# Fewer and larger transfers on the SP queue of an attention-then-mixture kernel, and V's transposed copy loaded one pair sooner

## The chip, the cores and the metric

One core of one Trainium2 chip runs the whole kernel as one program. The metric is the device time of one execution in microseconds (us), measured without the profiler, as the median of several runs. One further execution was profiled; all rows below come from it.

## The reference

Causal attention over 8 batches of 12 heads, 448 positions, head size 64; its rows (3584 tokens of 768 numbers) go through a mixture of 8 experts. Each token goes to the expert with its largest gate logit, each expert keeps its 80 tokens of highest gate weight, and all other rows of the output are zero.

```python
scores = q @ k.T / 8                      # (8, 12, 448, 448), causal mask
attn = exp(scores - max) / (sum + 1e-9)
x = (attn @ v) as rows of (8*448, 12*64)
logits = x @ w_gate                        # 8 experts
e = argmax(logits); g = softmax(logits)[e]
for each expert: its at most 80 tokens of largest g:
    out[token] = g * (relu(x[token] @ w1[e]) @ w2[e])     # 768 -> 1024 -> 768
```

## The kernel before

**Attention** runs over 48 pairs of heads (8 batches of 6 pairs; the two heads of a pair lie on partitions 0 to 63 and 64 to 127). The loop over pairs `i` has 8 slots `k`, and `CYCLE` writes down what each slot issues: the scores of pair `i` (`sp`, TensorE), their masking and minimum (`ns`, `nb`, VectorE), the exponentials (`prob`, ScalarE), the transposes of pair `i-1` (`tp`, copied to `PT`), the product with the values of pair `i-2` (`xo`, scaled to `xr` by VectorE in slot 5), and the store of pair `i-3` (`st`, slot 0) into the scratch tensor `xs`. Everything runs in the order in which it is written (`manual_schedule`), on each engine by itself. A group of three pairs is a half batch (`PH` = 3).

**Loads.** `load_pair` brings q and k of pair `i+4` in slot 0, each as its own transfer, into the raw tile `qk` (three pairs in rotation, `RING`); `split_pair` on GpSimd (POOL) makes two 16-bit parts of pair `i+3` in slot 6 (L344 a cast, L346 two subtractions). `load_values` brings the values `vt` of the next half batch. `load_turned` brings V a second time, with positions along the free dimension (`vT`): 672 KB in each of the pairs `p` = 4 and 5 of a batch, for the batch after the next.

**What vT is for.** The gate's logits come out of the attention product itself: V times the gate weights (`gp`, L377, TensorE) is put beside V. For a batch from the third on, this product is planned in the batch before it, with `gp0` in pair 1, slot 4 and `gp1` in pair 2, slot 4 (`FOLD`: 12 and 20 slots). There is one `vT` tile, so its next load waits for `gp1`. For the second batch, `FOLD_SECOND` plans `gp1` in pair 4, slot 4 of the first (36 slots).

**The turn of a batch.** Choosing the experts and ranking the tokens of batch `b` is spread over the two batches behind it (`STEPS`, in slots after the batch's end). At 55 comes `rank` (POOL), at 59 `rr` (VectorE, reads `rank`), at 60 `tn` (TensorE, reads `rr`) and then `tab` (VectorE, reads `tn`). Slot 60 is pair 1, slot 4 as well, so on TensorE `gp0` stands right ahead of `tn`, and `tn` right ahead of the scores of the next pair. This text calls that place the turn.

**Fill.** From pair 5 on, slots 1, 4 and 7 each issue one more transfer: a part of a piece of the expert weights (`piece_parts`, 192 or 256 KB, tile `wraw`) or, when no piece is due (`LOADS`), 64 zero rows of the output (`zero_rows`, 192 KB, out of the zero columns of `mask`).

**The queue.** Nearly all transfers are issued by SP in one program order, 414 of them. They take eight completion semaphores in turn (DMAHW0 to DMAHW7), so each issue first waits until the transfer eight before it has landed.

**The end.** `TAIL` orders the last values, gate and ranking steps; `close` clears the three tiles `xg0` to `xg2`, which take the gathered rows. Then the experts run, with weights in 1.5 MB transfers, and each expert's rows are scattered into the output.

Of the kernel before, what the change touches and what calls it, by code (L numbers as in the profile page):

```python
# [7 lines left out]
F32 = mybir.dt.float32  # L8
# [9 lines left out]
P = 128  # L18
DH = 64
# [3 lines left out]
TILES = 7  # L23
# [18 lines left out]

TAIL = """
st v0 ta tb rest2 ya yb sums0 lgp0 rows0 st0 rest6 v1 turned close rest4 sums1 lgp1 piece logit shifted raised *2 chosen rows1
st1 sums one_hot wsum one_zero wmore columns r0t r0c *3 weight weighted parts hold rl r1t r1c *1 lt cp ro
c3w c3l c2w c2l c1w gt3 *2 c0w c1l gt2 *1 c0l *1 gt1 places *1 earlier gt0 places_more own *5 rank rr tn tab *28
"""

# [2 lines left out]
def attention_then_moe(  # L51
    ctx: ExitStack,
    tc: tile.TileContext,
    qT: bass.AP,
    kT: bass.AP,
    v: bass.AP,
    vT: bass.AP,
    wg: bass.AP,
# [4 lines left out]
    capacity: int,  # L63
):
    nc = tc.nc
    B, _, NP, S = qT.shape
    N, D = out.shape
    E = wg.shape[2]
    F = w1.shape[3]
# [18 lines left out]
    spool = sel_stack.enter_context(tc.tile_pool(name="sel", bufs=2, side="right"))  # L88
# [38 lines left out]
    for r in range(2):  # L127
        x = akeep.tile([P, P * sum(CHUNKS)], F32, name=f"prob{r}")
# [7 lines left out]
    PH = NP // HB  # L136
    v_bufs = []
    for r in range(2):
        t = akeep.tile([P, NT, 2 * PH * VW], F32, name=f"vt{r}")
# [11 lines left out]
    PW = 3072  # L151
# [23 lines left out]
    wmore = [wearly]  # L175
# [21 lines left out]
    def piece_parts():  # L197

        got = []
        k = PIECES[len(wload)][3]  # L200
        got.append(piece())
        half = PW // k // 2

        def part(j, x):
            t, src = got[0]
            nc.sync.dma_start(t[:, j, x * half:(x + 1) * half], src[:, j, x * half:(x + 1) * half])
        return [lambda j=j, x=x: part(j, x) for j in range(k) for x in range(2)]


    presplits = [], [], []  # L210
# [25 lines left out]
    for r in range(2):  # L236
        t = akeep.tile([P, NT, H, E + 1], F32, name=f"fold{r}")
# [4 lines left out]
    zero = mask[:, 0:D // 2]  # L242
    zdone = [0]
    xg_bufs = []
# [68 lines left out]
    def zero_rows():  # L313

        r0 = zdone[0]
        n = min(P // 2, N - r0)
        nc.sync.dma_start(out[r0:r0 + n, :].rearrange("r (h c) -> (r h) c", h=2), zero[0:2 * n, :])
        zdone[0] += n


# [1 line left out]
    lo, hi = slice(0, DH), slice(DH, P)  # L322

    def raw_of(i):

        x = qk_raw[:, i % RING * 2 * S:(i % RING + 1) * 2 * S]
        return x, x[:, 0:S], x[:, S:2 * S]
# [5 lines left out]

    def load_pair(i):
        b, p = divmod(i, NP)
        _, q, k = raw_of(i)
        nc.sync.dma_start(q, qT[b, :, p, :])
        (nc.sync if i else nc.scalar).dma_start(k, kT[b, :, p, :])

    def split_pair(i):  # L340

# [16 lines left out]
    def load_turned(b, p0, p1):  # L358

        if b not in turned_values:  # L360
            turned_values[b] = akeep.tile([P, NP, S], F32, name="vT")
        nc.sync.dma_start(turned_values[b][:, p0:p1, :], vT[b, :, p0:p1, :])
# [111 lines left out]
    def values_group(pr):  # L474
        st = state[pr.b * HB + pr.p // PH]
        p = pr.p % PH

        def work():
            xo = pr.xo = ps_u.tile([P, 2, 512], F32, name="xo", tag="u")[:, 0, 0:TILES * VW].rearrange("k (t w) -> k t w", w=VW)
# [26 lines left out]
                                    in1=pr.r.unsqueeze(2).to_broadcast([P, TILES, E]), op=ALU.mult)  # L506

        def rows():
            xr = pr.xr = spool.tile([P, TILES, DH], F32, name="xr", tag="xr", bufs=4)
            nc.vector.tensor_tensor(out=xr, in0=pr.xo[:, :, 0:DH], in1=pr.r.unsqueeze(2).to_broadcast([P, TILES, DH]),  # L510
                                    op=ALU.mult)

        def store():
            xr = pr.xr
            r0, c0 = pr.b * S, pr.p * P
            nc.sync.dma_start(xs[r0:r0 + NO * P, c0:c0 + P].rearrange("(t k) d -> k t d", k=P),
                              xr[:, 0:2 * NO, :].rearrange("k (t j) d -> k t (j d)", j=2))
            for j, of in enumerate((lo, hi)):
                nc.sync.dma_start(xs[r0 + NO * P:r0 + S, c0 + j * DH:c0 + (j + 1) * DH], xr[of, TILES - 1, :])
        return work, sums, logits, rows, store  # L520

    NO = NT - 1
# [378 lines left out]
    with tc.manual_schedule():  # L901
# [25 lines left out]
        for i, pr in enumerate(pairs):  # L927
# [17 lines left out]
            for k in range(SLOTS):  # L945
# [15 lines left out]
                    load_values((i + 1) // PH)  # L961
                if i == 2 and k in (2, 5):
                    load_turned(1, k - 2, k + 1)
                if bt.b < B - 2 and k == 6 and pr.p >= NP - 2:
                    load_turned(bt.b + 2, 3 * (pr.p - NP + 2), 3 * (pr.p - NP + 3))

                if i == n - 2 and k == 0 and len(wload) >= WBUF and not parts:
                    load_piece()
# [3 lines left out]
                        f()  # L972
                        todo.remove(f)

                if i > 4 and k in (1, 4, 7):
                    if not parts and len(wload) < WBUF and (not PRE or i >= LOADS[len(wload)]):
                        parts = piece_parts()
                        if len(wload) <= PRE:
                            presplit(len(wload) - 1)
                    if parts:  # L980
                        parts.pop(0)()
                    elif zdone[0] < N:
                        zero_rows()
# [31 lines left out]
        def close():  # L1015
            att.close()
            wmore.append(ctx.enter_context(tc.tile_pool(name="wmore1", bufs=1, reuse_waits="tile")))
            xg_pool = ctx.enter_context(tc.tile_pool(name="xg", bufs=1, reuse_waits="tile"))
            for i in range(3):
                t = xg_pool.tile([SL, D], F32, name=f"xg{i}")  # L1020
                (nc.gpsimd if i else nc.vector).memset(t, 0.0)
                xg_bufs.append(t)
        steps["close"] = close

        def keep_warm(times):
# [342 lines left out]
```

## Time and profile before

| | |
|---|---|
| median of 3 runs | 456.21 us (454.61 to 457.66) |
| profiled execution | 456.73 us, span of its records 455.0 us |
| attention, about | 0 to 320 us |
| last ranking and first gather, about | 320 to 346 us |
| experts, about | 346 to 455 us |
| TensorE, VectorE, ScalarE, GpSimd busy | 398.4, 354.3, 341.0, 223.6 us |

Times in rows are us from the start of the span. A stretch's DMA share is the mean busy share of the core's 16 DMA engines. In a timeline, the bracket behind a row is the time that the engine sat idle ahead of it and what ended it.

### The profile page before, as it was taken

The page shows a single profiled execution, that of the slowest core. Times are in us where ns is not written, and L with a number is a line of the kernel's source. Part 1 is how long each engine was busy: PE and PEld are TensorE (multiplying, and loading weights), DVE is VectorE, ACT ScalarE, POOL GpSimd, SP SyncE. Part 2 cuts the span into 40 slices and gives each one's busy share as a digit, 9 for nine tenths or more (in the row PEclk, how much of TensorE's full clock was granted, in tenths as well). Part 3 has the DMA queues.
Part 4 walks back from the last instruction along what each step waited for, and adds up shares of the span by engine and source line. Part 5 has one row for each costly group of instructions (what it writes and reads, how often), then busy time and mean ns, then how long its engine had stood idle before and what let it go on. Part 6 is the DMA issues. An engine that isn't in the chain of part 4 may idle for free.

```text
span 455.0 us, 21917 instructions
## 1 busy us (share of the span) xinstructions
PE 398.4 (88%) x9186; PEld 350.8 (77%) x9187; DVE 354.3 (78%) x1321; ACT 341.0 (75%) x622; POOL 223.6 (49%) x362
## 2 busy tenths in 40 slices
PE   5699889798969989995997998898697889999994
PEld 3488778687848868883887787788367889999993
DVE  5366789687947879883698679988776999999792
ACT  5589779778848887982797688885744599897791
POOL 5665567477757857675675565631160241200002
PEclk9999999999979999996899899999699999999998
DMA  8948988979988798998889796456539999999911
GB/s 290 363 139 265 284 249 264 321 224 287 282 287 269 229 325 248 295 264 279 283 265 296 253 292 192 136 167 210 169 100 351 409 396 395 388 414 426 408 46 43
DMA packets 66034, 122.89 MB, mean 270 GB/s; under 512 B 13282, under 2 KB 54242, under 8 KB 62608
## 3 DMA queue, kind: packets, MB, share of 16 engines
q1 hardware_dynamic: 64736, 117.76, 76.1%
q0 software_dynamic: 1056, 3.51, 2.5%
q8 instruction: 72, 1.18, 1.1%
q14 instruction: 26, 0.21, 0.1%
q10 hardware_dynamic: 144, 0.23, 0.1%
HBM read 97.91 MB, written 23.99 MB: 268 GB/s over the span
## 4 chain that ended last, share of the span: by engine, by line
PE 53%; DMA 19%; DVE 13%; issue 6%; POOL 4%; SPq 3%; ACT 0%; POOLq 0%; DVEq 0%
PE xo L485 11%; PE sp L431 9%; DMA vT<-v_d 8%; PE tp L463 6%; DMA xs<-xr 5%; DVE ns L441 5%; PE op L1167 3%; PE op L1159 3%; PE hp L1173 3%; PE hp L1174 3%; PE hp L1171 3%; DMA xg<-xs,idx 3%; PE gp L377 2%; DMA qk<-k_t 2%; POOL qk L346 2%
## 5 line engine op out<-in xcount | busy, mean ns | idle before, releaser
L448 ACT ACTIVATE prob<-ns,nb 128x448 f32<-128x448 f32 (+6 forms) x336 | 145.1, 500 | 29.8 <-DVE nb L441 29.3
L441 DVE CUSTOM_DVE_ANT_0 ns<-sp,mask 128x448 f32<-128x448 f32 (+6 forms) x336 | 123.5, 420 | 33.5 <-PE sp L431 27.9
L485 PE MATMUL xo<-vt,PT 128*64 128x73 f32 x3072 | 113.8, 231 | 8.3 <-issue 3.8
L485 PEld LDWEIGHTS xo<-vt,PT 128*64 128x64 f32 x3072 | 105.6, 139 | 15.2 <-issue 5.5
L470 ACT COPY PT<-tp 128x1024 f32<-128x1024 f32 x92 | 88.8, 1015 | 22.8 <-PE tp L463 20.8
L346 POOL TENSOR_TENSOR qk<-qk,qk 128x448 f16<-128x448 f32 x90 | 92.9, 1053 | 3.7
L1084 DVE SCALAR_TENSOR_TENSOR wl<-wraw,wh 128x768 f16<-128x768 f32 (+1 forms) x87 | 89.1, 1080 | 3.7 <-ACT wh L1102 2.8
L431 PE MATMUL sp<-qk 64*64 64x128 f16 (+8 forms) x1974 | 72.0, 291 | 14.4 <-DMA qk<-k_t 4.3
L1102 ACT ACTIVATE wh<-wraw 128x768 f16<-128x768 f32 (+1 forms) x87 | 76.2, 940 | 4.2 <-PE hp L1174 2.2
L431 PEld LDWEIGHTS <-qk 64*64 64x64 f16 x1890 | 51.6, 111 | 20.8 <-issue 7.0
L463 PE MATMUL tp<-ident,prob 64*128 64x64 f32 x1536 | 59.8, 227 | 4.6 <-issue 3.9
L463 PEld LDWEIGHTS tp<-ident,prob 64*128 64x128 f32 x1536 | 52.6, 140 | 9.3 <-issue 4.4
L344 POOL CAST qk<-qk 128x896 f16<-128x896 f32 x45 | 42.0, 933 | 27.7 <-DMA qk<-k_t 23.5
L1260 POOL DMA_INDIRECT out<-yo,idx x8 | 9.8, 1225 | 71.5 <-ACT yo L1257 67.2
L1174 PEld LDWEIGHTS <-wl 128*128 128x128 f16 x378 | 37.7, 100 | 2.3 <-issue 1.5
L1173 PE MATMUL hp<-xl,wh 128*128 128x80 f16 x336 | 37.1, 202 | 1.4 <-issue 1.4
L1171 PEld LDWEIGHTS <-wh 128*128 128x128 f16 x378 | 38.0, 101 | 0.0
L1173 PEld LDWEIGHTS <-wh 128*128 128x128 f16 x378 | 37.8, 100 | 0.0
L1174 PE MATMUL hp<-xh,wl 128*128 128x80 f16 x336 | 37.1, 202 | 0.0
L1171 PE MATMUL hp<-xh,wh 128*128 128x80 f16 x336 | 37.1, 202 | 0.0
L377 PE MATMUL gp<-vT,wgd 128*32 128x224 f32 x192 | 19.7, 386 | 13.8 <-DMA vT<-v_d 12.4
L1119 POOL DMA_INDIRECT xg<-xs,idx x8 | 15.6, 1953 | 30.1 <-PE xtp L1137 14.3
(174 smaller groups left out, 599.0 us busy)
## 6 DMA issues: line engine op xcount, KB each, us to landing
wraw<-w SPq DMA_DIRECT2D x25, 1536.0 KB, 13.6
qk<-q_t SPq DMA_DIRECT2D x48, 224.0 KB, 4.0
out<-mask SPq DMA_DIRECT2D x56, 192.0 KB, 4.7
qk<-k_t SPq DMA_DIRECT2D x47, 224.0 KB, 4.1
vt<-v_t SPq DMA_DIRECT2D x16, 657.0 KB, 6.3
vT<-v_d SPq DMA_DIRECT2D x14, 672.0 KB, 6.7
xs<-xr SPq DMA_DIRECT2D x48, 192.0 KB, 4.8
wraw<-w SPq DMA_DIRECT2D x30, 256.0 KB, 5.4
```

The costliest lines, as they stand in the source:

```text
L346: nc.gpsimd.tensor_tensor(out=l[:, part], in0=x[:, part], in1=h[:, part], op=ALU.subtract)
L431: nc.tensor.matmul(pr.sp[t][to], q[rows, t * QB:(t + 1) * QB], k[rows, 0:WIDTH[t]], start=(x == 0), stop=(x == len(terms) - 1), skip_group ...
L441: nc.vector.tensor_tensor_reduce(out=ns[:, 0:w], in0=pr.sp[t], in1=mask[:, S - w:S], scale=-1.0 / 8.0, scalar=HUGE, op0=ALU.add, op1=ALU.m ...
L448: nc.scalar.activation(pr.P[:, OFF[t]:OFF[t] + w], ns[:, 0:w], AF.Exp, bias=nb, scale=-1.0)
L463: nc.tensor.transpose(tp[0][:, r, at:at + QB], pr.P[rows, off:off + P], ident[rows, rows])
L470: nc.scalar.copy(pr.PT[:, g], got[0])
L485: nc.tensor.matmul(xo[rows, slot, :], pr.PT[:, g, r, at:at + QB], st["vt"][:, c, (2 * p + j) * VW:(2 * p + j + 1) * VW], start=(rows.start ...
L1084: return nc.vector.scalar_tensor_tensor(out=l, in0=src, scalar=SW, in1=h, op0=ALU.mult, op1=ALU.subtract)
L1102: nc.scalar.activation(h, src, AF.Copy, scale=SW)
L1171: nc.tensor.matmul(o, wh[:, ws], ah[:, c, :], start=(x == 0 and i % per == 0), stop=False, skip_group_check=True)
L1173: nc.tensor.matmul(o, wh[:, ws], al[:, c, :], start=False, stop=False, skip_group_check=True)
L1174: nc.tensor.matmul(o, wl[:, ws], ah[:, c, :], start=False, stop=(x == n - 1), skip_group_check=True)
```

## The change

- q and k of a pair lie side by side in one input, and one transfer of 448 KB brings both (pair 0 still takes two, on two queues).
- The last 64 rows of a pair's positions are stored for three pairs at once, in two transfers of 48 KB behind every third pair, where each pair had two of 16 KB; the last three pairs keep their own. `xr` is a tile of three pairs in two copies, where it was one pair in four.
- `zero_rows` writes 128 rows in one transfer, and a part of a weight piece is no longer halved. The fill comes in slot 1 of each pair and slot 5 of each second one, half as often as before.
- `load_turned` comes at `p` = 3 and 4, where it was 4 and 5.
- VectorE clears `xg0` behind `parts` in the tail (`clear`), where it did so in `close`.

SP issues 256 transfers, where it issued 414. The other engines' order is the same but for `clear` and for one cast of the weights (`wh`) on ScalarE in the tail, which stands behind the two copies of `ex` and no longer ahead of them.

```diff
--- before.py
+++ after.py
@@ -42,7 +42,7 @@
 
 TAIL = """
 st v0 ta tb rest2 ya yb sums0 lgp0 rows0 st0 rest6 v1 turned close rest4 sums1 lgp1 piece logit shifted raised *2 chosen rows1
-st1 sums one_hot wsum one_zero wmore columns r0t r0c *3 weight weighted parts hold rl r1t r1c *1 lt cp ro
+st1 sums one_hot wsum one_zero wmore columns r0t r0c *3 weight weighted parts clear hold rl r1t r1c *1 lt cp ro
 c3w c3l c2w c2l c1w gt3 *2 c0w c1l gt2 *1 c0l *1 gt1 places *1 earlier gt0 places_more own *5 rank rr tn tab *28
 """
 
@@ -51,8 +51,7 @@
 def attention_then_moe(
     ctx: ExitStack,
     tc: tile.TileContext,
-    qT: bass.AP,
-    kT: bass.AP,
+    qkT: bass.AP,
     v: bass.AP,
     vT: bass.AP,
     wg: bass.AP,
@@ -63,7 +62,7 @@
     capacity: int,
 ):
     nc = tc.nc
-    B, _, NP, S = qT.shape
+    B, _, NP, S = vT.shape
     N, D = out.shape
     E = wg.shape[2]
     F = w1.shape[3]
@@ -199,12 +198,12 @@
         got = []
         k = PIECES[len(wload)][3]
         got.append(piece())
-        half = PW // k // 2
+        half = PW // k
 
         def part(j, x):
             t, src = got[0]
             nc.sync.dma_start(t[:, j, x * half:(x + 1) * half], src[:, j, x * half:(x + 1) * half])
-        return [lambda j=j, x=x: part(j, x) for j in range(k) for x in range(2)]
+        return [lambda j=j, x=x: part(j, x) for j in range(k) for x in range(1)]
 
 
     presplits = [], [], []
@@ -313,8 +312,11 @@
     def zero_rows():
 
         r0 = zdone[0]
-        n = min(P // 2, N - r0)
-        nc.sync.dma_start(out[r0:r0 + n, :].rearrange("r (h c) -> (r h) c", h=2), zero[0:2 * n, :])
+        n = min(P, N - r0)
+        x = 2 if n == P else 1
+        n = n if x == 2 else min(n, P // 2)
+        nc.sync.dma_start(out[r0:r0 + n, :].rearrange("(x r) (h c) -> (r h) x c", x=x, h=2),
+                          zero[0:2 * n // x, :].unsqueeze(1).to_broadcast([2 * n // x, x, D // 2]))
         zdone[0] += n
 
 
@@ -333,9 +335,11 @@
 
     def load_pair(i):
         b, p = divmod(i, NP)
-        _, q, k = raw_of(i)
-        nc.sync.dma_start(q, qT[b, :, p, :])
-        (nc.sync if i else nc.scalar).dma_start(k, kT[b, :, p, :])
+        if i:
+            nc.sync.dma_start(raw_of(i)[0], qkT[b, :, p, :])
+        else:
+            for queue, x, part in zip((nc.sync, nc.scalar), raw_of(i)[1:], (slice(0, S), slice(S, 2 * S))):
+                queue.dma_start(x, qkT[b, :, p, part])
 
     def split_pair(i):
 
@@ -474,6 +478,7 @@
     def values_group(pr):
         st = state[pr.b * HB + pr.p // PH]
         p = pr.p % PH
+        last_half = pr.b == B - 1 and pr.p >= NP - PH
 
         def work():
             xo = pr.xo = ps_u.tile([P, 2, 512], F32, name="xo", tag="u")[:, 0, 0:TILES * VW].rearrange("k (t w) -> k t w", w=VW)
@@ -506,17 +511,21 @@
                                     in1=pr.r.unsqueeze(2).to_broadcast([P, TILES, E]), op=ALU.mult)
 
         def rows():
-            xr = pr.xr = spool.tile([P, TILES, DH], F32, name="xr", tag="xr", bufs=4)
+            if not p:
+                st["xr"] = spool.tile([P, PH, TILES, DH], F32, name="xr", tag="xr", bufs=2)
+            xr = pr.xr = st["xr"][:, p]
             nc.vector.tensor_tensor(out=xr, in0=pr.xo[:, :, 0:DH], in1=pr.r.unsqueeze(2).to_broadcast([P, TILES, DH]),
                                     op=ALU.mult)
 
         def store():
-            xr = pr.xr
             r0, c0 = pr.b * S, pr.p * P
             nc.sync.dma_start(xs[r0:r0 + NO * P, c0:c0 + P].rearrange("(t k) d -> k t d", k=P),
-                              xr[:, 0:2 * NO, :].rearrange("k (t j) d -> k t (j d)", j=2))
-            for j, of in enumerate((lo, hi)):
-                nc.sync.dma_start(xs[r0 + NO * P:r0 + S, c0 + j * DH:c0 + (j + 1) * DH], xr[of, TILES - 1, :])
+                              pr.xr[:, 0:2 * NO, :].rearrange("k (t j) d -> k t (j d)", j=2))
+            many = 1 if last_half else PH if p == PH - 1 else 0
+            c1 = c0 + P - many * P
+            for j, of in enumerate((lo, hi) if many else ()):
+                nc.sync.dma_start(xs[r0 + NO * P:r0 + S, c1:c0 + P].rearrange("k (p h d) -> k p h d", d=DH, h=2)[:, :, j, :],
+                                  st["xr"][of, p + 1 - many:p + 1, TILES - 1, :])
         return work, sums, logits, rows, store
 
     NO = NT - 1
@@ -961,8 +970,8 @@
                     load_values((i + 1) // PH)
                 if i == 2 and k in (2, 5):
                     load_turned(1, k - 2, k + 1)
-                if bt.b < B - 2 and k == 6 and pr.p >= NP - 2:
-                    load_turned(bt.b + 2, 3 * (pr.p - NP + 2), 3 * (pr.p - NP + 3))
+                if bt.b < B - 2 and k == 6 and pr.p in (PH, PH + 1):
+                    load_turned(bt.b + 2, PH * (pr.p - PH), PH * (pr.p - PH + 1))
 
                 if i == n - 2 and k == 0 and len(wload) >= WBUF and not parts:
                     load_piece()
@@ -972,7 +981,7 @@
                         f()
                         todo.remove(f)
 
-                if i > 4 and k in (1, 4, 7):
+                if i > 4 and (k == 1 or k == 5 and i % 2):
                     if not parts and len(wload) < WBUF and (not PRE or i >= LOADS[len(wload)]):
                         parts = piece_parts()
                         if len(wload) <= PRE:
@@ -1018,8 +1027,10 @@
             xg_pool = ctx.enter_context(tc.tile_pool(name="xg", bufs=1, reuse_waits="tile"))
             for i in range(3):
                 t = xg_pool.tile([SL, D], F32, name=f"xg{i}")
-                (nc.gpsimd if i else nc.vector).memset(t, 0.0)
+                if i:
+                    nc.gpsimd.memset(t, 0.0)
                 xg_bufs.append(t)
+            steps["clear"] = lambda: nc.vector.memset(xg_bufs[0], 0.0)
         steps["close"] = close
 
         def keep_warm(times):
@@ -1349,8 +1360,7 @@
         return np.ascontiguousarray(a.reshape(B, H // 2, 2, S, d).transpose(0, 2, 4, 1, 3)).reshape(B, 2 * d, H // 2, S)
 
     arrays = {
-        "q_t": by_pair(q),
-        "k_t": by_pair(k),
+        "qk_t": np.concatenate([by_pair(q), by_pair(k)], axis=3),
         "v_t": by_half(v),
         "v_d": by_pair(v),
         "wg": np.ascontiguousarray(moe_w_gate.reshape(D // P, P, E).transpose(1, 0, 2)),
```

**SP, the second batch's pairs 4 and 5 (before).** It begins with the first half of `vT` for the fourth batch. `xs<-xr` are stores, `vt` values; the bracket names what the issue waits for, DMAHW being the turn of the eight semaphores.

```order
L362 DMA vT<-v_d 128x1344 [waits DMAHW5_49,PE_49]
L206 DMA wraw<-w 128x512 [waits DMAHW6_49]
L516 DMA xs<-xr 128x3x128 [waits DMAHW7_49,DVE_49]
L519 DMA xs<-xr 64x64 [waits DMAHW0_49]
L519 DMA xs<-xr 64x64 [waits DMAHW1_49]
L337 DMA qk<-q_t 128x448 [waits DMAHW2_49,Pool_49]
L338 DMA qk<-k_t 128x448 [waits DMAHW3_49]
L354 DMA vt_103<-v_t 128x1314 [waits DMAHW4_49,PE_49]
L356 DMA vt_103<-v_t 64x438 [waits DMAHW5_49,PE_49]
L206 DMA wraw<-w 128x512 [waits DMAHW6_49]
L206 DMA wraw<-w 128x512 [waits DMAHW7_49]
L362 DMA vT<-v_d 128x1344 [waits DMAHW0_49]
```

**SP, the same batch from its pair 3 on (after).** It begins with the same half of `vT`.

```order
L366 DMA vT<-v_d 128x1344 [waits DMAHW0_49,PE_49]
L522 DMA xs<-xr 128x3x128 [waits DMAHW1_49,DVE_49]
L339 DMA qk<-qk_t 128x896 [waits DMAHW2_49,Pool_49]
L205 DMA wraw<-w 128x1024 [waits DMAHW3_49]
L366 DMA vT<-v_d 128x1344 [waits DMAHW4_49]
L522 DMA xs<-xr 128x3x128 [waits DMAHW5_49,DVE_49]
L527 DMA xs<-xr 64x3x64 [waits DMAHW6_49]
L527 DMA xs<-xr 64x3x64 [waits DMAHW7_49]
L339 DMA qk<-qk_t 128x896 [waits DMAHW0_49,Pool_49]
L358 DMA vt_103<-v_t 128x1314 [waits DMAHW1_49,PE_49]
```

The second half of `vT` stands ahead of the store that opens pair 5 and ahead of the load of `vt`, where it stood behind both, and three transfers lie between the two halves, where ten did.

**SP, the first batch's pairs 3 and 4 (before).** Loads of `qk` for pairs 7 and 8, the store of pair 1, and the first half of `vT` for the third batch.

```order
L337 DMA qk<-q_t 128x448 [waits DMAHW1_49,Pool_49]
L338 DMA qk<-k_t 128x448 [waits DMAHW2_49]
L516 DMA xs<-xr 128x3x128 [waits DMAHW3_49,DVE_49]
L519 DMA xs<-xr 64x64 [waits DMAHW4_49]
L519 DMA xs<-xr 64x64 [waits DMAHW5_49]
L337 DMA qk<-q_t 128x448 [waits DMAHW6_49,Pool_49]
L338 DMA qk<-k_t 128x448 [waits DMAHW7_49]
L362 DMA vT<-v_d 128x1344 [waits DMAHW0_49,PE_49]
```

**SP, the same place (after).**

```order
L339 DMA qk<-qk_t 128x896 [waits DMAHW1_49,Pool_49]
L366 DMA vT<-v_d 128x1344 [waits DMAHW4_49,DMAHW7_49,DMAHW2_49,PE_49]
L522 DMA xs<-xr 128x3x128 [waits DMAHW3_49,DVE_49]
L339 DMA qk<-qk_t 128x896 [waits DMAHW5_49,Pool_49]
L366 DMA vT<-v_d 128x1344
L522 DMA xs<-xr 128x3x128 [waits DMAHW6_49,DVE_49]
L527 DMA xs<-xr 64x3x64
```

That half of `vT` with its wait for TensorE (`PE_49`) now stands ahead of the store of pair 1 and of the load of pair 8, where it stood behind them.

**VectorE, the tail, around the last `r` (before).** `rr` and `logit` are ranking and gate steps, `xg` the tile for gathered rows.

```order
L718 TENSOR_TENSOR rm<-ro_8625,slots_e 80x320
L774 TENSOR_TENSOR rr<-rank,slots_t 128x320
L1021 MEMSET xg_8786 80x768
L501 TENSOR_SCALAR r<-xo 128x7
L502 RECIPROCAL r<-r 128x7
L505 TENSOR_TENSOR lgp<-xo,r 128x56
L531 TENSOR_REDUCE logit<-lgp 128x24
```

**VectorE, the same place and the end of `parts` (after).**

```order
L727 TENSOR_TENSOR rm<-ro_8437,slots_e 80x320
L783 TENSOR_TENSOR rr<-rank,slots_t 128x320
L506 TENSOR_SCALAR r<-xo 128x7
L507 RECIPROCAL r<-r 128x7
L510 TENSOR_TENSOR lgp<-xo,r 128x56
L540 TENSOR_REDUCE logit<-lgp 128x24
...
L633 TENSOR_TENSOR grest<-gow,mv 128x32
L634 TENSOR_TENSOR mv<-grest,mv 128x4x8
L1033 MEMSET xg_8597 80x768
L700 TENSOR_SCALAR lt,lower_8695<-rl,ggw 128x80 x4
```

The clearing of `xg` leaves the place ahead of the last `r` and stands between the last part and `lt`.

## Rows read from the trace of the kernel before

**Rows 1.** Busy time by stretch: us, PE, PEld, DVE, ACT, POOL, PEclk, DMA, GB/s.

```profile
83.00:251.00 168.00, 145.36 (x3683) 124.86 (x3684) 128.34 (x612) 125.16 (x239) 112.03 (x183) 0.94 0.88 277
346.00:455.00 109.00, 99.45 (x1956) 98.28 (x1956) 92.49 (x117) 84.53 (x137) 18.46 (x12) 0.98 0.82 329
```

**Rows 2.** Waits of PE and of DVE, 45 to 320 us: total, times, longest.

```profile
PE gp L377 <- DMA vT<-v_d: 12.4, 4, 5.4
...
DVE rr L774 <- POOL rank L755: 11.6, 6, 5.2
```

**Rows 3.** Timeline of PE at four turns.

```profile
88.91 1.60 PE L377 MATMUL gp<-vT,wgd 128*32 128x224 f32 x8 [2.04 <-DMA vT<-v_d]
...
130.59 1.70 PE L377 MATMUL gp<-vT,wgd 128*32 128x224 f32 x8 [3.66 <-DMA vT<-v_d]
...
170.16 0.94 PE L377 MATMUL gp<-vT,wgd 128*32 128x224 f32 x8 [1.33 <-DMA vT<-v_d]
...
211.36 1.70 PE L377 MATMUL gp<-vT,wgd 128*32 128x224 f32 x8 [5.41 <-DMA vT<-v_d]
```

**Rows 4.** Timeline of SP's issues in the second batch, 72 to 82 us.

```profile
72.84 0.38 SPq L362 DMA_DIRECT2D vT<-v_d  x1
...
73.79 0.38 SPq L516 DMA_DIRECT2D xs<-xr  x1
...
81.75 0.44 SPq L362 DMA_DIRECT2D vT<-v_d  x1
```

**Rows 5.** DMA issues of the page: count, KB each, median us to landing.

```profile
qk<-q_t SPq DMA_DIRECT2D x48, 224.0 KB, 4.0
...
qk<-k_t SPq DMA_DIRECT2D x47, 224.0 KB, 4.1
...
vT<-v_d SPq DMA_DIRECT2D x14, 672.0 KB, 6.7
...
xs<-xr SPq DMA_DIRECT2D x96, 16.0 KB, 4.2
```

**Rows 6.** Timeline of DVE at the same four turns.

```profile
90.93 0.20 DVE L798 CAST tab<-tn 80x40 bf16<-80x40 f32 x1 [2.04 <-PE tn L787]
92.37 0.62 DVE L441 CUSTOM_DVE_ANT_0 ns<-sp,mask 128x448 f32<-128x448 f32 x1 [1.25 <-PE sp L431]
...
133.25 0.20 DVE L798 CAST tab<-tn 80x40 bf16<-80x40 f32 x1 [2.37 <-PE tn L787]
...
134.69 0.63 DVE L441 CUSTOM_DVE_ANT_0 ns<-sp,mask 128x448 f32<-128x448 f32 x1 [1.25 <-PE sp L431]
...
172.58 0.62 DVE L441 CUSTOM_DVE_ANT_0 ns<-sp,mask 128x448 f32<-128x448 f32 x1 [0.31 <-PE sp L431]
...
209.51 0.68 DVE L774 TENSOR_TENSOR rr<-rank,slots_t 128x160 bf16<-128x160 f16 x2 [5.17 <-POOL rank L755]
...
214.02 0.20 DVE L798 CAST tab<-tn 80x40 bf16<-80x40 f32 x1 [1.25 <-PE tn L787]
215.46 0.62 DVE L441 CUSTOM_DVE_ANT_0 ns<-sp,mask 128x448 f32<-128x448 f32 x1 [1.25 <-PE sp L431]
```

**Rows 7.** Timelines of SP and POOL ahead of the fourth of these turns.

```profile
198.30 2.05 SPq L337 DMA_DIRECT2D qk<-q_t  x1
...
205.73 0.93 POOL L344 CAST qk<-qk 128x896 f16<-128x896 f32 x1 [4.08 <-DMA qk<-k_t]
```

**Rows 8.** Timeline of DVE in the tail.

```profile
318.54 0.70 DVE L1021 MEMSET xg<- 80x768 f32 x1
...
325.29 0.30 DVE L691 TENSOR_SCALAR_CACHE_REDUCE lt<-rl,ggw 128x80 bf16<-128x80 f32 x1 [0.91 <-PE rl L685]
```

**Rows 9.** Timelines of SP and POOL in the first batch.

```profile
30.75 0.53 SPq L337 DMA_DIRECT2D qk<-q_t  x1
...
35.39 0.33 SPq L362 DMA_DIRECT2D vT<-v_d  x1
...
40.23 0.93 POOL L344 CAST qk<-qk 128x896 f16<-128x896 f32 x1
```

## The prediction, made before the changed kernel was run

> **What bounds the kernel now.** I read the busy time by stretch first. From 83 to 251 us TensorE is busy for 145 of 168 us, VectorE for 128, and the DMA engines for 0.88 of the time [rows 1]. So three resources are near full, TensorE is the fullest, and some 23 us of it are idle. The experts' stretch keeps its work under this change. I then read what the idle time waits for. On TensorE, from 45 to 320 us, the largest single item is the product `gp` waiting for `vT`, 12.4 us in four waits; on VectorE it is `rr` waiting for `rank` on POOL, 11.6 us in six [rows 2]. Both stand at the turn of a batch, so I read the four turns one by one. TensorE waits there 2.04, 3.66, 1.33 and 5.41 us [rows 3]. The reader is to see in the SP timeline why: the second half of `vT` is asked for at 81.75 us, 8.0 us behind the store that opens its pair (73.79) and 8.9 behind the first half [rows 4]; a half takes a median of 6.7 us to land [rows 5], so it is there at about 88.5, and `gp` goes on at 88.91.
>
> **What an earlier vT is worth.** In the new order the second half stands ahead of the store of pair 5, whose issue was at 73.79 [rows 4]. Asked for at 73.8 at the latest it lands at about 80.5, over 8 us ahead of 88.91, and the longest of the four waits is 5.41 [rows 3]. I take all four waits as gone. They are not worth 12.4 us, because VectorE has work of its own at a turn (`rr`, the last `xr`, the logits of the batch). What the kernel gets back is what VectorE stood idle for behind `gp`: its waits for `tn` ahead of `tab` and for the scores ahead of `ns`. First turn 2.04 + 1.25 = 3.3 us; second 2.37 + 1.25 = 3.6; third 0.3, since VectorE was late there by itself; fourth 1.25 + 1.25 = 2.5 [rows 6]. Sum 9.7 us. Next late is VectorE, by its own work.
>
> The fourth turn has a second cause. `rr` waited 5.17 us for `rank` [rows 6], because POOL, in its order, stood at the cast of a `qk` that had not landed, for 4.08 us [rows 7]. That load's issue alone took 2.05 us on SP at 198.30 [rows 7], where an issue without a wait takes about 0.5 (0.53 at 30.75 [rows 9]), so it stood for its semaphore's turn. The change leaves 158 of 414 issues out; 25 of those that stay belong to the experts. Per pair that is 389/48 = 8.1 before and 231/48 = 4.8 after, so the eight transfers in flight reach back over 1.7 pairs, where it was one. Bounds for this: 0 (the load lands as late as before) to 4.1 us (the whole wait). I take 2.0, the wait of the issue that this row shows, nearer to the middle.
>
> **Fewer transfers.** The 158 issues at about 0.5 us are nearly 80 us of SP's time, and none of it is on the path: SP stands at the store of each pair until `xr` is there. What counts is landing. For q and k together the trace has no row, so I bound it. 224 KB take 4.0 us and 672 KB take 6.7 [rows 5], which puts 448 KB at 4.0 + 2.7 x 224/448 = 5.35 us from its issue (an estimate from these rows). Before, k was issued 0.6 us behind q and landed 4.1 later [rows 5, 9], 4.7 in all. So the pair may come 0.7 us later, or, when the transfer no longer queues behind its own half and behind the small stores, earlier by up to the same. Most pairs don't feel it; a turn does, through POOL. At three turns that is 2.1 us at worst; I charge 1.0.
>
> [...]
>
> Three pairs' last rows in one store: nobody reads them before the gather, and the last half batch keeps single stores, so it costs nothing at the end. VectorE's write of `xr` for the first pair of a half batch now waits for the stores of the half batch two back, which are asked for three pairs earlier, some 17 us, and a 16 KB store lands in 4.2 [rows 5]: nothing; if that cover were gone, VectorE would wait in every third pair. The zero rows and weight parts keep their bytes per pair.
>
> **vT past the first batch's loads.** For the third batch the earlier request is a new block: `vT` must wait for `gp1` of pair 4. SP did reach it at 35.39, behind that product [rows 9]. Now it stands in front of the store of pair 1 and the load of pair 8 (30.75 before [rows 9]), and these move to about 36.2. Pair 8 then lands at about 41.5 (5.35 us), and POOL's cast of it was at 40.23 [rows 9]: 1.3 us late. POOL's parts of pair 8 are read by TensorE in pair 8, two pairs behind that cast, over 10 us, and the split itself takes three. So nothing on the path; without that cover 1.3 us.
>
> **The tail.** `xg0`'s clearing is 0.70 us of VectorE at 318.54, with the last `r` behind it; its new place is an idle gap of 0.91 us ahead of `lt` [rows 8]. Gain 0.7, no less than 0, if POOL's own clearing slows it.
>
> **Sum.** 9.7 + 2.0 + 0.7 - 1.0 = 11.4 us less. Against the profiled execution that is 456.7 - 11.4 = 445.3; the median of the runs is 0.5 us lower, and I say 445.0 us. A difference of 1% of this time, 4.6 us, is about what a measurement of this kernel can tell from none.
>
> **Rivals.**
>
> *The DMA engines become the bound.* Their work from 83 to 251 us is 0.88 x 168 = 148 us [rows 1]. With 11 us taken out of that stretch their share would be 148/157 = 0.94. If they can't be filled so far, loads of `qk` come late at ordinary turns, and VectorE gets back only about a third of the 9.7 us. For it: the fourth turn was already of this kind [rows 7]. Against it: `vT`'s bytes are spread better, and no bytes are added. Time: 456.2 - 3.2 - 0.7 = about 452.
>
> *The lighter queue gives more.* The transfers double in size, and if they also moved faster the DMA engines would be the looser resource. The experts' stretch, with 1.5 MB transfers, moves 329 GB/s at a share of 0.82, 401 per full share; attention moves 277 at 0.88, 315 [rows 1]. At a rate in between, all of POOL's 4.1 us come back, the charge of 1.0 goes, and some of the rest of `rr`'s 11.6 us (11.6 - 5.2 = 6.4, of which I give half) [rows 2]: 9.7 + 4.1 + 0.7 + 3.2 = 17.7, so 438.5. Against it: 672 KB transfers ran in the same slow stretch. [...]
>
> *Slower: larger transfers in front of qk.* A weight part of 512 KB or 384 KB of zeros can now stand as one block ahead of a load that POOL needs, eight such in flight instead of eight of half the size. If each of five turns then waits as the fourth did, 5.17 us [rows 6], where the six waits had a mean of 1.9 [rows 2], five turns cost 5 x 3.2 = 16 us, against 9.7 and 0.7 gained: 456.2 + 16.2 - 10.4 = 462. It decides if loads of `qk` regularly land over 7.3 us behind the moment when SP turns to them, as that one did (198.30 to about 205.6 [rows 7]). Against it: the load of `qk` comes ahead of its pair's fill, and the fill comes half as often.
>
> *The early request isn't early.* If SP were held at the store as long as before, `vT` would come as late. The order speaks against it. Time: 456.
>
> **How the numbers follow.** Forecast (441 to 449) 0.54; DMA-bound (449 to 455) 0.19; more (436 to 441) 0.13; slower 0.09 (458 to 466); not early 0.05. The range of 8 in 10 leaves out the slower case and the far half of "more": 438.5 to 455. Faster by over 1% (under 451.6): forecast, "more" and some of the DMA-bound case, 0.72; within 1%: 0.19; slower 0.09.
>
> **What the profile after would show.** Right: no wait of `gp` for `vT` over 0.3 us; `tab` and `ns` at a turn behind VectorE's own work; SP's share of issue time down by a third or more; `xg` no longer ahead of the last `r`. Right but smaller: POOL's casts waiting longer for `qk`, a DMA share near 0.94. Wrong: `rr` waiting over 4 us at several turns, or TensorE idle on something not in this list, such as a store of `xr` or pair 8's parts near 50 us.

## The result: 455.42 us, less than half of the gain forecast

| | before | after |
|---|---|---|
| median of 20 runs | 456.94 us (452.48 to 463.40) | 455.42 us (447.70 to 465.01) |
| profiled execution, its span | 456.73, 455.0 us | 449.94, 448.2 us |
| TensorE's mean granted clock in the profiled execution | 0.954 | 0.988 |

The ratio of after to before is 0.9891, interval 0.985 to 0.9932. This ratio, here and in the tables below, compares only the executions within 1.5% of the fastest of their kernel, since the others run longer (in after at a granted clock of 0.963 to 0.978, where those within it have 0.979 to 0.988): 16 of 20 before (median 456.21 us) and 7 of 20 after (451.14 us); over all executions the medians differ by 0.3%. Forecast were 445.0 us (438.5 to 455.0) and a gain of 2.5%; by the ratio the gain is 1.1%, and the median lies just outside the range. The profiled execution of after lies 5.5 us under its median, so its rows show where time goes, not how much the change is worth on average.

**The waits that were to go are gone.** TensorE of after, from 45 to 320 us: what it waited for, in total, times, longest, against [rows 2]:

```profile
PE xo L490 <- issue: 14.1, 13, 2.9
PE sp L435 <- issue: 6.5, 6, 2.2
PE sp L435 <- DVE xr L517: 4.0, 6, 0.9
PE tp L467 <- issue: 3.8, 3, 1.4
PE gp L381 <- issue: 2.6, 2, 1.7
```

There is no wait for `vT` where there were 12.4 us. On VectorE, same stretch, what is left of the two waits of the turn, which were 11.6 us for `rr` in [rows 2] and up to 2.37 us a time for `tab` in [rows 6]:

```profile
DVE tab L807 <- PE tn L796: 2.7, 2, 1.8
...
DVE rr L783 <- POOL rank L764: 0.7, 4, 0.2
```

**Another wait took their place.** In the rows of TensorE above four of five end with "issue": the profile shows nothing that the engine waits for. What it lacks is its next instruction, as shown below. They add up to 27.0 us. The same view of before has them too, below the rows shown in [rows 2]; I passed over them:

```profile
PE tp L463 <- issue: 3.9, 2, 2.2
PE xo L485 <- issue: 3.8, 5, 1.4
PE sp L431 <- issue: 2.0, 3, 1.3
...
PE rl L685 <- issue: 0.2, 1, 0.2
```

That is 9.9 us. So 12.4 us of waiting for `vT` went and 17.1 us of issue waits came.

**What the gain is made of.** Busy time from 45 to 312 us, before and then after (columns as in [rows 1]):

```profile
45.00:312.00 267.00, 235.39 (x6102) 203.69 (x6101) 209.79 (x993) 208.49 (x397) 167.18 (x278) 0.96 0.83 262
```

```profile
45.00:312.00 267.00, 232.49 (x6187) 201.56 (x6176) 215.69 (x1001) 208.31 (x398) 166.24 (x279) 0.99 0.81 265
```

TensorE is idle for 267 - 235.4 = 31.6 us before and for 34.5 us after: its idle time did not fall at all. It got through 85 more products because each took 232.49/6187 = 37.6 ns and not 38.6, at a granted clock of 0.99 and not 0.96. One nanosecond on the 7231 products outside the experts (9187 - 1956) is 7.2 us, about the 6.8 us between the two spans. The pages agree: for the same products TensorE is busy for 398.4 us before and 389.9 after, and its idle time over the span rose by 1.7 us. Where the clock was lost before, its windows show, behind the long waits at the second and fourth turn of [rows 3]:

```profile
130.00:134.00 4.00, 3.41 (x32) 2.04 (x36) 0.99 (x5) 0.47 (x2) 1.36 (x4) 0.50 0.97 324
134.00:138.00 4.00, 4.00 (x94) 3.74 (x88) 3.17 (x19) 2.56 (x6) 2.19 (x3) 0.65 0.70 228
...
212.00:216.00 4.00, 4.00 (x55) 2.81 (x55) 1.42 (x6) 0.47 (x2) 2.51 (x5) 0.50 0.78 247
216.00:220.00 4.00, 4.00 (x90) 3.74 (x83) 2.84 (x21) 2.56 (x6) 1.71 (x5) 0.66 0.90 305
```

Behind 3.66 and 5.41 us without work the clock is at 0.50, the lower of the two values, 1.0 and 0.5, that the clock records of both traces hold. Summed over windows of 2 us from 45 to 312 us, the shortfall of the clock is 12.0 us before and 1.7 after. The new waits, of 2.9 us at most, mostly leave the clock where it is: in this stretch of after it falls once, for 3.4 us at 246.6 us. The length of a single stop does not settle it, since in the trace of before it also fell for 3.4 us behind the 2.04 us of the first turn.

**Fewer transfers.** DMA issues of the page of after, against [rows 5]: count, KB each, median us to landing.

```profile
qk<-qk_t SPq DMA_DIRECT2D x47, 448.0 KB, 5.0
out<-mask SPq DMA_DIRECT2D x28, 384.0 KB, 6.5
...
vT<-v_d SPq DMA_DIRECT2D x14, 672.0 KB, 7.3
xs<-xr SPq DMA_DIRECT2D x48, 192.0 KB, 3.7
```

And the longest of SP's own waits from 45 to 320 us, before and then after:

```profile
SPq L516 <- DVE xr L510: 13.8, 6, 3.9
```

```profile
SPq L522 <- DVE xr L517: 95.2, 29, 5.6
```

With the waits that the view puts down to other steps of VectorE, SP stood at this store for 35 us before and for 140 after. Before, it was behind its program most of the time. Now it is ahead, stands at the store of each pair, and puts out all that follows in one run.

**Where TensorE's instructions come from.** The page lists a DMA queue of its own, `q8 instruction: 72, 1.18, 1.1%`: 72 packets, 1.18 MB, 16 KB each. TensorE has 2 x 9187 records of products and weight loads, 255 per packet, so a packet is 256 of its instructions; the page counts the time of these packets, that 1.1%, on the same 16 DMA engines as the data's (75.2% for the queue of SP's transfers). The trace's packet times, set against the stops: in after a packet landed at 78.81, 113.47, 205.22 and 233.18 us, and TensorE goes on 1.3 to 1.4 us later each time. The stops fall at one count, too. Number TensorE's instructions from the program's start, weight loads and semaphore instructions included: each of its products that waited over 0.4 us for issue from 45 to 312 us stands at 192 to 195 of a block of 256 (7 of 7 before, 22 of 22 after). No data wait would keep to that count. Two of these stops:

```profile
114.83 1.11 PE L490 MATMUL xo<-vt,PT 128*64 128x73 f32 x28 [2.89 <-issue]
...
206.52 0.57 PE L381 MATMUL gp<-vT,wgd 128*32 128x224 f32 x5 [1.70 <-issue]
```

The second is the fourth turn, where [rows 3] had 5.41 us for `vT`.

### The profile page after: what moved, and what is told of

Its sections match the earlier page's. It is cut to its first block, busy times and chain, and to the rows that moved or that the text cites. A ratio compares the mean times of both kernels' runs of the same rounds, so it can differ in the third digit from the quotient of the medians.

```text
span 448.2 us, 21724 instructions
## 1 busy us (share of the span) xinstructions
PE 389.9 (87%) x9187; PEld 344.4 (77%) x9187; DVE 357.6 (80%) x1321; ACT 340.5 (76%) x622; POOL 225.7 (50%) x362
## 3 DMA queue, kind: packets, MB, share of 16 engines
q1 hardware_dynamic: 53248, 117.75, 75.2%
q8 instruction: 72, 1.18, 1.1%
## 4 chain that ended last, share of the span: by engine, by line
PE 61%; DVE 14%; issue 10%; DMA 6%; POOL 5%; ACT 3%; POOLq 0%; SPq 0%; DVEq 0%; ACTq 0%
PE xo L490 18%; PE sp L435 10%; PE tp L467 8%; DVE wl L1095 3%; DVE ns L445 3%; DMA qk<-qk_t 3%; PE op L1178 3%; PE hp L1170 3%; POOL qk L350 3%; PE op L1170 2%; PE gp L381 2%; PE hp L1184 2%; PE hp L1185 2%; PE hp L1182 2%; PE wp L1040 2%
## 5 line engine op out<-in xcount | busy, mean ns | idle before, releaser
L490 PEld LDWEIGHTS xo<-vt,PT 128*64 128x64 f32 x3072 | 103.9, 136 | 26.5 <-issue 16.6
L435 PE MATMUL sp<-qk 64*64 64x128 f16 (+8 forms) x1974 | 70.9, 284 | 17.4 <-issue 6.5
L435 PEld LDWEIGHTS <-qk 64*64 64x64 f16 x1890 | 49.6, 108 | 24.3 <-issue 13.2
L467 PE MATMUL tp<-ident,prob 64*128 64x64 f32 x1536 | 58.8, 226 | 4.2 <-issue 3.8
L467 PEld LDWEIGHTS tp<-ident,prob 64*128 64x128 f32 x1536 | 51.7, 138 | 8.7 <-issue 4.2
L967 POOL COPY tie<-xr 128x1 f32<-128x1 f32 x43 | 8.9, 208 | 53.5 <-DVE xr L517 52.1
L1130 POOL DMA_INDIRECT xg<-xs,idx x8 | 18.2, 2270 | 26.3 <-PE xtp L1148 11.5
```

The costliest lines, as they stand in the source:

```text
L435: nc.tensor.matmul(pr.sp[t][to], q[rows, t * QB:(t + 1) * QB], k[rows, 0:WIDTH[t]], start=(x == 0), stop=(x == len(terms) - 1), skip_group ...
L467: nc.tensor.transpose(tp[0][:, r, at:at + QB], pr.P[rows, off:off + P], ident[rows, rows])
L490: nc.tensor.matmul(xo[rows, slot, :], pr.PT[:, g, r, at:at + QB], st["vt"][:, c, (2 * p + j) * VW:(2 * p + j + 1) * VW], start=(rows.start ...
```

## The experiments

The ratio is each kernel's time over that of before on the same chip, with its interval; "issue" is the sum of TensorE's issue waits in the profiled execution, 45 to 312 us (9.9 before, 27.0 after; the same kernel as after, run once more as `whole`, gives 26.4). Each profile is one execution.

**Parts of the change, first four.** `vt_only` is before with the earlier request alone, `no_vt` is after without it:

```diff
-                if bt.b < B - 2 and k == 6 and pr.p >= NP - 2:
-                    load_turned(bt.b + 2, 3 * (pr.p - NP + 2), 3 * (pr.p - NP + 3))
+                if bt.b < B - 2 and k == 6 and pr.p in (PH, PH + 1):
+                    load_turned(bt.b + 2, PH * (pr.p - PH), PH * (pr.p - PH + 1))
```

`small_fill` is after with the fill as before (halved parts, 64 zero rows, slots 1, 4 and 7). `no_zero` is after without the zero rows:

```diff
-                    elif zdone[0] < N:
+                    elif False:
                         zero_rows()
...
-    while zdone[0] < N:
+    while False:
         zero_rows()
```

> The kernel before with vT loaded one pair sooner and nothing else. The whole change left TensorE without a wait for vT from 45 to 320 us, but its waits for issue, each of which ends about 1.2 us behind the landing of a 16 KB packet of its own instructions, grew from 10 to 27 us. Theory pace: TensorE, no longer held at the turns, uses up its instructions sooner, and the fetch is as slow as ever; then the waits for issue rise to over 20 us here too, and the time is that of the whole change, 0.985 to 0.993 of before. Theory bulk: the larger transfers hold up the fetch; then the waits for issue stay at 10 to 14 us here, and the time is 0.975 to 0.983 of before (9 to 11 us less).

> The whole change but for vT, which is asked for in the old place. Pace: some waits for vT come back (5 to 12 us), the waits for issue fall to 10 to 18 us, and the time is 0.99 to 1.00 of before. Bulk: the waits for issue stay over 20 us beside the waits for vT, and the time is 1.00 to 1.02 of before.

> The whole change, but weight parts and zero rows in transfers of the old size and in the old three slots of a pair. Pace: as the whole change, waits for issue over 20 us, 0.985 to 0.993 of before. Bulk: waits for issue 10 to 16 us, 0.970 to 0.982 of before.

> The whole change with the zero rows of the output left out: 11 of some 78 MB of traffic during attention go. If the fetch of instructions is held up by the data transfers, under either theory, the waits for issue fall to under 12 us in the stretch from 83 to 251 us where the zero rows went, and the time to 0.96 to 0.975 of before. A third theory, that TensorE's sequencer is the limit by itself, whatever the transfers do, expects them unchanged at 27 us, and 0.985 to 0.993.

| kernel | median us | ratio | issue us | wait for vT |
|---|---|---|---|---|
| vt_only | 460.72 | 1.0005 (0.9958 to 1.0052) | 18.3 | none |
| no_vt | 458.16 | 1.0023 (0.9917 to 1.0129) | 31.5 | none |
| small_fill | 449.65 | 0.9816 (0.9753 to 0.9878) | 23.1 | none |
| no_zero | 443.95 | 0.9652 (0.9579 to 0.9725) | 14.5 | none |

`vt_only` takes away exactly the waits that I had priced at 9.7 us, and it is worth nothing that can be told from zero. The first of TensorE's waits there, 45 to 312 us:

```profile
PE xo L485 <- issue: 8.3, 7, 2.0
PE sp L431 <- DVE xr L510: 7.1, 12, 1.1
PE sp L431 <- issue: 6.8, 6, 2.2
PE sp L431 <- DVE own L750: 3.3, 4, 1.2
PE tp L463 <- issue: 3.0, 2, 2.2
```

Of the 12.4 us that went, 8.4 came back as issue waits; waits for VectorE and ScalarE grew by 5.2, from 8.8 to 14.0. VectorE's own wait for `rank` stayed (13.8 us). `no_vt` shows that the waits also go with `vT` asked for as late in the program as before: with fewer issues SP gets there in time. Leaving out 11 MB of zeros takes the DMA share from 83 to 251 us from 0.86 to 0.74 and nearly halves the issue waits, the first sign that data traffic makes them. That is what both theories expected of `no_zero`; for the rest neither holds whole. `vt_only` lies outside both in time, `small_fill` has the issue waits of "pace" and a time just inside "bulk", and the waits for `vT` that both expected of `no_vt` are not there.

**A second stop of SP, and the parts alone.** If the transfers come in too thick a run, a second place per pair where SP must wait should help. `spread` is after with such a stop in slot 3 (POOL clears a column of 4 bytes per partition, SP stores one element of it), with the fill behind it:

```diff
+    def pace(i):
+        c = mark[:, i % 4:i % 4 + 1]
+        nc.gpsimd.memset(c, 0.0)
+        nc.sync.dma_start(marks[0:1, i % 4:i % 4 + 1], c[0:1, :])
...
-                if i > 4 and (k == 1 or k == 5 and i % 2):
+                if 4 < i < n - 2 and k == 3:
+                    pace(i)
+                if i > 4 and (k == 3 or k == 5 and i % 2):
```

The fill's first slot moves with it, from 1 to 3; no run moves the fill alone. `spread_small` has the stop with the small fill (slots 3, 5, 7). `fill_only` and `qs_only` are before with one part of the change each: the larger fill, or the merged q and k with the grouped last rows.

> The whole change, and in each pair SP has a second stop: a 4-byte transfer that waits for a memset of POOL behind its split of q and k, ahead of the pair's fill, so that a pair's transfers no longer go out in one run behind the store. No byte of the work is moved or left out. Theory depth (what holds up the fetch of TensorE's instructions is the bytes that stand in the DMA rings when it is asked for, and fewer, larger transfers let SP put in more at once): waits for issue from 45 to 312 us fall from 27 to under 18 us, and the time is 0.970 to 0.982 of before. Theory pace (TensorE has become too fast for a fetch that is as slow as ever): 23 to 30 us, and 0.985 to 0.995.

> As the run with the second stop, but weight parts and zero rows in transfers of the old size, three a pair, all behind the stop. Depth: the best of all, waits for issue under 16 us, 0.965 to 0.978. Pace: 0.980 to 0.990, as with the small fill alone.

> The kernel before with the larger weight parts and zero rows and nothing else. Depth: waits for issue over 15 us (9.9 before), and the waits for vT at the turns shrink, since SP has 51 issues less; 0.995 to 1.01. Pace: waits for issue stay near 10 as long as waits for vT are there, and the time falls by what the vT waits lose, 0.985 to 0.995.

> The kernel before with q and k in one transfer and the last rows stored for three pairs, and nothing else (fill, vT and the clearing of xg0 as before). Depth: part of the gain of the run with the small fill, which was 0.9816: vT waits under 4 us, waits for issue 15 to 25 us, 0.983 to 0.992. Pace: the same waits, but 0.99 to 1.0, since taking out waits for vT alone gave nothing.

| kernel | median us | ratio | issue us |
|---|---|---|---|
| spread | 444.71 | 0.9608 (0.9565 to 0.9650) | 21.0 |
| spread_small | 446.07 | 0.9671 (0.9619 to 0.9722) | 19.2 |
| fill_only | 452.52 | 0.9852 (0.9813 to 0.9891) | 22.0 |
| qs_only | 450.04 | 0.9776 (0.9721 to 0.9830) | 25.9 |

Neither part alone leaves a wait for `vT`, and each alone is worth as much as the whole change or more. I read this as parts that pay into the same purse, SP's lateness; what more they do was not separated. "Depth" had the direction of `spread` right, but not the size of its issue waits (under 18 us expected), and it had `fill_only` and `qs_only` slower than they came out. `spread` has the lowest ratio of the kernels that do all the work; the interval of `spread_small` overlaps with its own. SP now stands in two places:

```profile
SPq L249 <- POOL mark L248: 53.0, 22, 4.4
SPq L530 <- DVE xr L525: 24.8, 18, 3.7
```

**The same chip for all, and the stop elsewhere.** `whole` is after again, `spread_again` is spread again, `spread_novt` is spread with `vT` asked for where before asked, `stop_before` is before with the same stop (fill in slots 3, 5, 7).

> The whole change as it is, on the same chip as the three kernels beside it, so that they can be held against each other. 0.985 to 0.993 of before, waits for issue 22 to 32 us from 45 to 312 us, no wait for vT.

> The second stop of SP, beside the whole change. Theory depth: 0.955 to 0.972 of before and at least 1% below the whole change. Theory pace: the earlier result lay in the chip, and the two are within 0.7% of each other.

> The second stop with vT asked for in the old place. If the fewer transfers alone make vT early enough, as the run without the vT move had it, no wait for vT over 0.5 us and the time of the run with the stop within 0.7%. If the stop, which holds the fill and vT back, makes vT late again, 4 to 10 us of waits for vT and 1 to 2% above the run with the stop.

> The kernel before with the second stop and its fill behind it, nothing else: 414 transfers and the stops. Theory depth with a full queue: SP has no time left there (it waits for xr only 14 us of 275), so the stop makes all later transfers late, waits for vT and rank of 25 us and more, 1.00 to 1.03 of before. If the stop helps by itself, whatever the number of transfers: 0.97 to 0.99.

| kernel | median us | ratio | issue us |
|---|---|---|---|
| whole | 457.47 | 0.9863 (0.9805 to 0.9921) | 26.4 |
| spread_again | 443.19 | 0.9636 (0.9569 to 0.9703) | 21.9 |
| spread_novt | 447.59 | 0.9692 (0.9604 to 0.9780) | 18.7 |
| stop_before | 466.12 | 1.0144 (1.0073 to 1.0215) | 11.8 |

On one chip the stop makes the change 0.9636/0.9863 = 0.977 of itself, 2.3% faster. On the kernel before it costs 1.4%: SP has little time to spare there, and waits for `vT` grow to 21.7 us. The earlier request is worth little either way (0.9636 against 0.9692, intervals overlapping). All four came out as expected in time.

**The instruction fetch by itself.** These four kernels leave the whole computation out. TensorE does 4096 products of the form of `xo` with no data to wait for, and SP loads q and k into buffers that nobody reads, as many under way as there are buffers. Each ran once:

```python
for i in range(LOADS_N):              # 0, 110, 110, 220
    t = pool.tile([P, W // CUT], F32, name="load", tag="load", bufs=DEPTH)
    ...
    nc.sync.dma_start(t, qkT[b, :, p, x:x + W // CUT])
for i in range(4096):
    h = slice(i % 2 * 64, i % 2 * 64 + 64)
    nc.tensor.matmul(xo[h, 0:73], a[:, h], vt, start=True, stop=True, skip_group_check=True)
```

> This kernel leaves the whole computation out: TensorE does 4096 products of the form of xo, one behind the other and with no data to wait for, and SP puts no transfers out. Both theories: TensorE's instruction packets (16 KB, 256 instructions, one for every 128 products, about 4.6 us at the 36 ns of a product) land in about 2.5 us, in time; issue waits of TensorE under 1 us in all, some 147 us of products.

> The same products, and beside them 110 loads of 448 KB on SP's queue into two buffers that nobody reads, so at most 896 KB are under way. Theory (queued bytes delay the packets): landing about 3.3 us behind its request, which is just in time at 4.6 us a packet with 1.2 us from landing to going on; issue waits 0 to 8 us while the loads run. Rival (the issue waits of the attention stretch come from something else, its data waits or its mix of work): no issue waits here nor in the two deeper ones.

> The same with four buffers, so up to 1792 KB under way. Theory: landing 4.5 us or more behind the request, so that each packet costs TensorE 1 us or more: 30 or so packets, issue waits 20 to 60 us. Rival: none.

> The same with 220 loads of half the size into eight buffers: as many bytes under way as with four of 448 KB, in transfers as many as the kernel before uses. If the bytes under way decide, the issue waits are those of four of 448 KB, within a third; if the size of a transfer decides, under half of them.

| kernel | under way, at most | us | issue us | packet landing behind its mark, us |
|---|---|---|---|---|
| fetch_none | none | 267.76 | 0 | 1.38 |
| fetch_2x448 | 896 KB | 278.04 | 5.4 | 2.83 |
| fetch_4x448 | 1792 KB | 300.25 | 26.5 | 3.90 |
| fetch_8x224 | 1792 KB | 296.03 | 22.9 | 3.64 |

The mark is the start of instruction 193 of a block of 256; in `fetch_none` the packets' transfers start 0.04 to 0.73 us behind it. Of each kernel the means run over the packets between 20 and 138 us. Timeline of TensorE in `fetch_4x448`:

```profile
46.76 4.27 PE L45 MATMUL xo<-vt,a 128*64 128x73 f32 x128 [1.10 <-issue]
52.41 4.27 PE L45 MATMUL xo<-vt,a 128*64 128x73 f32 x128 [1.38 <-issue]
```

It stops behind every 128 records of products, which with their weight loads are 256 instructions; its trace has 64 packets of 16 KB for 8192 records of products. The numbers add up: a block lasts 4.05 us, and landing (3.90) and going on (1.4 behind it) make 5.3, some 1.2 us too late, about what one stop lasts (26.5 us in 23). I had expected a landing of 4.5 us or more. The rival of the expectations, that the issue waits come from the mix of work, falls: there is one kind of work here, and no wait without traffic. Half the transfer size at the same bytes gives 22.9 against 26.5 us, within the third that was set, so the bytes under way decide, and the size of a transfer hardly does. The DMA share rises along with them (0.75, 0.98 and 1.01 from 20 to 120 us); depth and fullness are not told apart here. The products took 262 us, not the 147 that I expected: each shows as two records of 32 ns, and I had counted one of 36.

## Why the prediction was wrong

**The step that failed** is the end of the part on `vT`: "I take all four vT waits as gone. [...] What the kernel gets back is what VectorE stood idle for behind `gp` [...] Sum 9.7 us. Next late is VectorE, by its own work." The first sentence came true. The rest did not: next late was TensorE's own instruction fetch (8.4 of the 12.4 us in `vt_only`), and only behind it the work of VectorE and ScalarE (5.2). The fetch was in the trace of before, 9.9 us of it in the same view as [rows 2], and my reading stopped at the largest two rows. `vt_only` prices the step: 1.0005 (0.9958 to 1.0052), nothing that can be told from zero where I had 9.7 us, 2.1%.

**Why the fetch got later.** Over 50 to 312 us, a packet of before lands 3.23 us behind its mark on average, 10 of 48 over 4.2 us; of after 3.73, 17 of 49. Over the 14 traces of the whole kernel together the landing grows with the bytes that SP has asked for and that have not begun at the mark: 2.8 to 3.1 us on average up to 700 KB, 4.1 from there to 1200 KB, 4.5 above (680 packets). Above 1200 KB are 4 of 48 packets before and 8 of 49 after, where SP issues a pair's transfers in one run. The fetch kernels show that step by itself. That the bunching of issues is what `spread` mends is shown only in part: its packets land 3.44 and 3.54 us behind their marks, earlier than after's and `whole`'s (3.73 both), and its issue waits of 21.0 and 21.9 us are 4.5 to 6 fewer, where I expected under 18. That is about half of the 2.3%, some 10 us, between `whole` and `spread_again`; the rest is open. The profiled executions can't settle it: from its 1000th to its 6900th product TensorE takes 252.2 us in after and 243.6 in `spread`, 5.9 of the difference in issue waits, but 250.0 in `whole` and 250.1 in `spread_again`, where against 4.5 us fewer issue waits stands a shortfall of the clock of 5.1 us, 1.7 in `whole` (45 to 312 us).

**A term that was missing on the other side** is the clock. I counted a wait as the time that it lasts. The second and the fourth turn also ran some 6 and 7 us behind theirs at half the clock (0.5 until 136.84 and 218.76 us in the clock records of before), and what the profiled execution gained is that: 7.2 us by the sum above. On one chip, the median granted clock over the executions was 0.960 for before and 0.974 for `whole`. How much of the 1.4% between the two is clock, no run here separates.

**The fourth turn, 2.0 us.** POOL no longer waits for `qk` at the cast ahead of that turn's `rank`, its 31st of this form in both traces:

```profile
198.72 0.94 POOL L348 CAST qk<-qk 128x896 f16<-128x896 f32 x1
```

Against 4.08 us in [rows 7] the whole wait went, not half of it, and `rr` lost 10.9 of its 11.6 us over all turns. The mechanism, SP's late issues, was right and larger than I made it. It would have removed the `vT` waits too, which I had put down to the order of the program: the order alone does it (`vt_only`), and so do fewer issues alone (`no_vt`, `qs_only`, `fill_only`). So my sentence that none of SP's 80 us of issues is on the path, since SP stands at the store of each pair, was wrong for before: it stood there for 35 of 275 us, and its lateness was on the path at the turns.

**Fewer transfers, -1.0.** The merged load lands after 5.0 us, against 5.35 estimated; POOL waits 8.7 us for `qk` in all (23.5 before), so the charge was none.

**Pair 8's load** came late as worked out (POOL's cast of it at 41.46 us behind a wait of 2.33), and nothing on the path followed. **The tail**: `xg0`'s clearing is in its new place, with no idle time left ahead of `lt`, against [rows 8]:

```profile
319.84 0.70 DVE L1033 MEMSET xg<- 80x768 f32 x1
320.64 0.30 DVE L700 TENSOR_SCALAR_CACHE_REDUCE lt<-rl,ggw 128x80 bf16<-128x80 f32 x1
```

From the end of `rr` ahead of the last `r` to `idx`'s first step it is 12.4 us where it was 14.2, so 0.7 was not too much.

**The rivals.** None of them happened as told. The nearest in time and in kind is the bound by the DMA engines (about 452 us): it had data late behind data, with a share of 0.94. The share is 0.86 from 83 to 251 us, `qk` is early, and what came late was the one small transfer in the same engines that no line of the kernel asks for. "The lighter queue gives more" fell on its premise: attention moves 280 GB/s at that share, 326 per full share, where it was 315 and the rival wanted a rate between that and 401. Where the prediction said what would prove it wrong, "TensorE idle on something not in this list" is what happened.

In `fetch_none` the fetch cost TensorE nothing (0 us of issue waits in a span of 266.0); at 1.8 MB under way, in `fetch_4x448`, it cost 26.5 us in 298.5.

## What to carry to other kernels

Before crediting a removed wait, list every other wait of the engine that is to profit, "issue" among them, and ask what it will run short of when it no longer stops; and count the clock that a long stop costs behind it as well as the stop (here 0.5 for some 6 and 7 us behind stops of 3.66 and 5.41). A load that comes late on an in-order issue queue may be late through the number of issues ahead of it: here each edit that thinned them took the 12.4 us of waits for `vT` to none, and their gains did not add up. Fewer and larger transfers may want a stop between them, where the queue has time to spare: here it gave 2.3% on top of the change, and cost 1.4% where there was little to spare.

## What the runs showed of the hardware

TensorE's instructions arrive as 16 KB packets (72 in after) on the DMA engines that the data use, 1.1% of those engines' span. With nothing else there a packet lands 1.38 us behind the mark, beside 1.8 MB of queued loads after 3.6 to 3.9, and 256 instructions of a dense stretch last 4.05 us. TensorE goes on behind the landing by 1.2 to 1.6 us in nine of ten of the 272 stops over 0.4 us, 1.4 at the median. Executions of one kernel differ by up to 17 us (447.70 to 465.01 of after), in part with the granted clock: over its 20 runs 0.01 of clock goes with 4.6 us.
